# Weight conversion of a one-core attention and MLP kernel: the shifted first words go through a PSUM bank

## The chip, the cores and the metric

The kernel runs on one core of a Trainium2 chip. The metric is the device time of one execution in microseconds (us); smaller is better. PE is TensorE (matmuls), DVE is VectorE, ACT is ScalarE, POOL is GpSimd, SP is the engine that only issues transfers.

## The reference

```python
q_s = exp(q - max(q, -1)); q_s /= sum(q_s, -1) + 1e-9         # 8 batches, 8 heads, 576 rows, 64 wide
k_s = exp(k - max(k, 2));  k_s /= sum(k_s, 2) + 1e-9
x = q_s @ (k_s.T @ v)                                          # heads side by side: (8, 576, 512)
xn = (x - mean(x)) / sqrt(var(x) + 1e-6) * g_ln
x = x + relu(xn @ w_ch1) @ w_ch2                               # w_ch1 (512, 2048), w_ch2 (2048, 512): float64
# then 4 heads of causal attention on x, the two best of 4 by a gate weighted, each through wo
```

What matters here is that the two MLP weights arrive as float64, while the engines compute in float32. Each weight has to be turned into a pair of float32 halves (a rounded high part and the rest) before its matmuls.

## The kernel before

**Weights.** The class `Wide` takes the float64 weights as pairs of int32 words. One block is 128 partitions by 512 values (512 KB); there are 32 blocks, two for each of the 16 slices `f` of the hidden layer (`w1_f`, `w2_f`). A block is loaded by SP into `wraw` (L230) and goes through seven pieces (`pieces`, L234 to L271):

- `size` (ACT, L246): the second word, scaled as a float32, gives `w_t`.
- `shift` (DVE, L250): `w_t` shifted left by 3, SBUF to SBUF, in place.
- `rest` (ACT, L253): the first word as a number, in place in `wraw`.
- `sign` (DVE, L256): the sign bit of the second word is put to `w_t`: two SBUF inputs, SBUF output.
- `whole` (POOL, L260): the rest is added, as an integer.
- `big` (ACT, L263) and `small` (DVE or POOL, L267): the two halves that the matmuls use.

`w_t` has 4 buffers, `wraw` has 4.

**Stages.** 24 blocks (f 0 to 11) are converted in the first stage, together with the attention of batches 0 and 1 in units of two heads (units 0 to 7: `k`, `q`, `km`, `sm`, `pkm`, `pq`, `pkv`, `po`), two layer norms for each of the two batches (`pmu`, `pvar`, `xc`, `xhl`), and the 24 MLP steps of batch 0. A step is 12 matmuls into `psh` (L174), a split into halves `hh` by ACT (L708) and DVE (L711), and 12 matmuls into four `acc` banks; after the last step of a half row block DVE adds `acc` to `xT` (L729). The other 8 blocks (f 12 to 15) are converted in a later round, near 636 to 713 us, while the MLP of batches 6 and 7 runs.

**Order.** In the first stage a planner (`plan`) orders all engines: every piece is an `Op` with an engine, a cost in ns and what it depends on, and takes places in rings (buffers). Of the ops that could start soonest on an engine it takes the one with the earliest due time. An op that takes the ring `y` makes the ops up to its release due at once (`rush`). The order that comes out is then fixed on PE, DVE, ACT and POOL; each engine works strictly in that order. In the later rounds a scheduler of the language orders the engines.

**PSUM.** `psy` gives a bank out of two with the tag `y`; at the start it also hands out three of the `acc` banks in turn, until the first layer norm has read its mean (`spare.clear`). The attention's transposes and products and the layer norm's means live in these banks.

```python
c0 = A(0, ACT, 520, g(0), [at.get(("w", k - 1, 0)), ld])
c1 = A(1, DVE, 340, g(1), [c0])
c2 = A(2, ACT, 520, g(2), [c0])
c3 = A(3, DVE, 600, g(3), [c1])
```

Of the kernel before, what the change touches and what calls it, by code (L numbers as in the profile page):

```python
# [9 lines left out]
I32 = mybir.dt.int32  # L10
U32 = mybir.dt.uint32
AF = mybir.ActivationFunctionType
ALU = mybir.AluOpType
# [116 lines left out]
def tile_kernel(ctx: ExitStack, tc: tile.TileContext, q, k, v, g_ln, w1, w2, w_gate, wq, wk, wv, wo, out):  # L130
    nc = tc.nc
    w1, w2 = w1.bitcast(I32), w2.bitcast(I32)
    B, H, S, D = q.shape
    DM = H * D
# [21 lines left out]
    def raw(ap):  # L156
        return ap.bitcast(F32)
# [15 lines left out]
    def mm(o, lhsT, rhs, start, stop):  # L173
        nc.tensor.matmul(o, lhsT, rhs, start=start, stop=stop)  # L174
# [39 lines left out]
    class Wide:  # L214
# [18 lines left out]
        def pieces(self):  # L233

            r, h, lo = self.now()
            n = self.at
            self.at += 1
            low, high = r[:, :, 0], r[:, :, 1]  # L240
            box = []

            def size():
                t = self.pool_t.tile([P, DM], I32, tag="t", name="w_t", bufs=TB)
                box.append(t)
                nc.scalar.activation(t.bitcast(F32), high.bitcast(F32), AF.Copy, scale=REBASE)  # L246

            def shift():
                t = box[0]
                nc.vector.tensor_scalar(t, t, 3, None, op0=ALU.logical_shift_left)  # L250

            def rest():
                nc.scalar.activation(low, low.bitcast(U32), AF.Copy, scale=2.0 ** -29)  # L253

            def sign():
                nc.vector.scalar_tensor_tensor(box[0], high, -0x80000000, box[0], op0=ALU.bitwise_and,  # L256
                                               op1=ALU.bitwise_or)

            def whole():
                nc.gpsimd.tensor_tensor(box[0], box[0], low, op=ALU.add)  # L260

            def big():
                nc.scalar.activation(h, box[0].bitcast(F32), AF.Copy)  # L263

            def small():
                eng = nc.vector if n in CDVE else nc.gpsimd
                eng.tensor_tensor(lo, box[0].bitcast(F32), raw(h), op=ALU.subtract)  # L267
                while len(self.tiles) < min(n + 1 + self.ahead, len(self.blocks)):
                    self.load()

            return size, shift, rest, sign, whole, big, small  # L271

        def now(self):
# [44 lines left out]
    def psy(name):  # L318
        if spare:

            spare.append(spare.pop(0))
            if spare[-1] is not None:
                return ps_acc.tile([P, 512], F32, tag=spare[-1], name=name)
        return ps_y.tile([P, 512], F32, tag="y", name=name)
# [5 lines left out]
    def unit_pool(n):  # L330
        return ap0 if n in (2, 3) else ap
# [7 lines left out]
    for i in range(NPR):  # L339
        t = unit_pool(i).tile([P, NCH, 2, D + 2], F32, tag=f"v{i}", name=f"v{i}", bufs=1)  # L340
        nc.gpsimd.memset(t[:, :, :, D:], 1.0)
        vbuf.append(t)
        t = unit_pool(i).tile([P, P], F32, tag=f"kvw{i}", name=f"kvw{i}", bufs=1)
        nc.gpsimd.memset(t, 0.0)
        kvwhole.append(t)
    for i in range(2):
        t = ap.tile([P, 2, P], F32R, tag=f"kv{i}", name=f"kv{i}", bufs=1)
# [475 lines left out]
    def start():  # L823


        PE_, ACT, DVE, POOL, SP = ENG.PE, ENG.Activation, ENG.DVE, ENG.Pool, ENG.SP
        ops, at, live = [], {}, []

        def add(name, eng, cost, fn, deps=(), lat=LAT):
            op = at[name] = Op(eng, cost, fn, deps, lat)  # L830
            ops.append(op)
            return op
# [165 lines left out]
        for k in range(nblocks):  # L998
            box = []
            live.append(box)  # L1000
            A = lambda nm, eng, cost, fn, deps: add(("w", k, nm), eng, cost, fn, deps)

            def one(i, box=box):
                if not box:
                    box.extend(wide.pieces())
                box[i]()

            g = lambda i, one=one: (lambda: one(i))
            ld = add(("w", k, "ld"), SP, 1450, wide.load, [at.get(("w", k - 1, "ld"))], lat=1100)
            c0 = A(0, ACT, 520, g(0), [at.get(("w", k - 1, 0)), ld])  # L1010
            c1 = A(1, DVE, 340, g(1), [c0])
            c2 = A(2, ACT, 520, g(2), [c0])
            c3 = A(3, DVE, 600, g(3), [c1])
            c5 = c4 = A(4, POOL, 1220, g(4), [c2, c3])
            c6 = A(6, ACT, 520, g(5), [c4])
            c7 = A(7, *((DVE, 600) if k in CDVE else (POOL, 1220)), g(6), [c6, at.get(("w", k - 1, 7))])
            c0.take("t", c7)
            ld.take("raw", c5)
# [8 lines left out]
        for n, st in enumerate(steps):  # L1027
            u = Step(*st)
            b, h, f, f0, f1 = st[:5]
            live.append(u.__dict__)  # L1030
            A = lambda nm, eng, cost, fn, deps: add(("mm", n, nm), eng, cost, fn, deps)
# [57 lines left out]
    spare.extend(SPARE)  # L1089
    n0 = len(traced())  # L1090
    start()
    in_order(traced()[n0:])

# [521 lines left out]
```

## Time and profile before

| | us |
|---|---|
| median of 3 runs | 1356.46 (1353.22 to 1361.91) |
| the profiled execution | 1351.34 |
| its span, first to last instruction | 1349.5 |
| PE / DVE / ACT / POOL busy | 1298.5 / 872.3 / 688.5 / 342.9 |

The profile is of one execution. Its span is shorter than its time by 1.84 us, which lie around the instructions. Busy times of PE are modelled for overlapping matmuls; the granted clock says how fast TensorE was allowed to run.

### The profile page before, as it was taken

How to read it: one execution, taken by the hardware profiler on the slowest of the kernel's cores; microseconds unless marked ns; L12 is line 12 of the kernel's file. 1: busy time of each engine (PE TensorE's matmuls, PEld its weight loads, DVE VectorE, ACT ScalarE, POOL GpSimd, SP SyncE). 2: the span in 40 equal slices, each digit the busy share in tenths (PEclk: the TensorE clock that was granted, in tenths of full speed). 3: DMA queues.
4: the chain of work that ended last, by engine and by line, in shares of the span. 5: the costliest groups of instructions: out<-in, count | busy, mean ns of one | idle time of the engine just before them, and what ended most of it. 6: DMA issues, size and time to landing. Idle time of an engine off the chain costs nothing.

```text
span 1349.5 us, 26838 instructions
## 1 busy us (share of the span) xinstructions
PE 1298.5 (96%) x9932; PEld 1257.0 (93%) x9932; DVE 872.3 (65%) x2570; ACT 688.5 (51%) x1802; POOL 342.9 (25%) x445
## 2 busy tenths in 40 slices
PE   5788999999999999999999999999999999999997
PEld 3677999999999999999999999999999999999995
DVE  7997565745646655556472247777768676776785
ACT  7786343434334433334442135656666656565666
POOL 5867123122131221212240002111212111121211
PEclk9799999999999999999999999999999999999999
DMA  9764232331322323315212033323232332422021
GB/s 229 217 189 123 76 112 56 117 95 45 110 75 98 89 70 110 76 53 156 64 34 47 1 96 111 105 82 107 89 91 90 93 96 66 121 79 85 23 67 56
DMA packets 136771, 124.84 MB, mean 93 GB/s; under 512 B 84160, under 2 KB 124096, under 8 KB 133056
## 3 DMA queue, kind: packets, MB, share of 16 engines
q1 hardware_dynamic: 126176, 97.16, 25.9%
q10 hardware_dynamic: 10464, 25.95, 5.2%
q8 instruction: 79, 1.29, 0.4%
q14 instruction: 52, 0.43, 0.1%
HBM read 74.07 MB, written 35.39 MB: 81 GB/s over the span
## 4 chain that ended last, share of the span: by engine, by line
PE 79%; DVE 9%; DMA 4%; ACT 3%; issue 2%; SPq 1%; POOL 1%; ACTq 0%; DVEq 0%; POOLq 0%
PE psh L174 25%; PE acc L174 19%; PE psqk L174 7%; PE psc L174 7%; PE pssc L174 4%; PE py L174 4%; PE psv L174 4%; PE pso L174 3%; PE pst L1400 2%; DMA q<-in_q_dram 2%; PE po L174 1%; DVE w_t L256 1%; DVE w_t L250 1%; DMA wraw<-in_moe_w_ch_dram 1%; DMA k<-in_k_dram 1%
## 5 line engine op out<-in xcount | busy, mean ns | idle before, releaser
L174 PE MATMUL psh<-xhl,w 128*128 128x288 f32 x3072 | 473.3, 299 | 2.2 <-DVE xhl L661 1.6
L174 PEld LDWEIGHTS psh<-xhl,w 128*128 128x128 f32 x3072 | 430.9, 190 | 5.8 <-DVE xhl L661 2.3
L174 PE MATMUL acc<-hh,w 128*128 128x288 f32 x2400 | 373.3, 300 | 9.6 <-DVE hh L711 8.7
L174 PEld LDWEIGHTS acc<-hh,w 128*128 128x128 f32 x2400 | 336.8, 190 | 15.2 <-DVE hh L711 12.4
L711 DVE SCALAR_TENSOR_TENSOR hh<-psh,hh 128x288 fp32r<-128x288 f32 x200 | 90.4, 452 | 153.4 <-ACT hh L708 152.3
L708 ACT ACTIVATE hh<-psh 128x288 fp32r<-128x288 f32 x200 | 81.8, 409 | 163.3 <-PE psh L174 155.6
L1388 POOL TENSOR_SCALAR sm<-sm,st,lg 128x128 f32<-128x128 f32 (+3 forms) x128 | 80.8, 641 | 273.7 <-DVE st L1385 99.3
L174 PE MATMUL psqk<-x,wqk 128*128 128x288 f32 x768 | 112.6, 298 | 0.5 <-DVE lg L1288 0.3
L174 PEld LDWEIGHTS psqk<-x,wqk 128*128 128x128 f32 x768 | 104.7, 188 | 1.8 <-PE pst L1400 0.8
L174 PE MATMUL psc<-hb,w 128*128 128x288 f32 x672 | 100.5, 299 | 0.0
L1376 ACT ACTIVATE sm<-sm,st 128x128 f32<-128x128 f32 (+2 forms) x144 | 83.7, 583 | 18.3 <-DVE st L1368 16.4
L174 PEld LDWEIGHTS psc<-hb,w 128*128 128x128 f32 x672 | 92.4, 189 | 0.3
L1419 ACT ACTIVATE aTh<-pst 128x128 fp32r<-128x128 f32 (+5 forms) x254 | 79.3, 335 | 24.3 <-PE pst L1400 11.9
L1368 DVE CUSTOM_DVE_ANT_0 sm<-pssc,mask 128x128 f32<-128x128 f32 (+2 forms) x144 | 67.6, 482 | 32.7 <-PE pst L1400 20.4
L1420 DVE TENSOR_TENSOR aTl<-pst,aTh 128x384 fp32r<-128x384 f32 (+4 forms) x222 | 82.0, 382 | 10.1 <-ACT aTh L1419 7.5
L473 POOL TENSOR_TENSOR qe<-q,sm 128x320 f32<-128x320 f32 x64 | 47.9, 769 | 99.5 <-PE pkv L512 93.7
L608 POOL TENSOR_TENSOR sq<-sq 128x288 f32<-128x288 f32 x45 | 37.0, 822 | 116.1 <-ACT sq L636 114.0
L174 PE MATMUL py<-aTh,vv 128*128 128x320 f32 (+4 forms) x228 | 58.4, 275 | 1.6 <-DVE yf L1472 0.9
L174 PE MATMUL pssc<-k,q 128*128 128x128 f32 (+3 forms) x256 | 58.0, 326 | 0.5 <-DVE st L1368 0.5
L422 POOL TENSOR_TENSOR q<-q,sm 128x640 f32<-128x640 f32 x28 | 35.8, 1278 | 85.7 <-DVE sm L419 85.5
L260 POOL TENSOR_TENSOR w_t<-w_t,wraw 128x512 int32<-128x512 int32 x32 | 46.1, 1443 | 40.6 <-issue 11.7
L419 DVE TENSOR_REDUCE sm<-q 128x10 f32<-128x640 f32 x32 | 26.1, 816 | 44.5 <-DMA q<-in_q_dram 44.5
(173 smaller groups left out, 2123.2 us busy)
## 6 DMA issues: line engine op xcount, KB each, us to landing
wraw<-in_moe_w_ch_dram SPq DMA_DIRECT2D x32, 512.0 KB, 3.8
xn_d<-xhl ACTq DMA_DIRECT2D x14, 1152.0 KB, 4.9
xhl<-xn_d SPq DMA_DIRECT2D x14, 1152.0 KB, 5.2
xp_d<-xT ACTq DMA_DIRECT2D x16, 576.0 KB, 3.5
k<-k SPq DMA_DIRECT2D x32, 288.0 KB, 3.5
k<-in_k_dram SPq DMA_DIRECT2D x32, 256.0 KB, 2.8
q<-in_q_dram SPq DMA_DIRECT2D x32, 256.0 KB, 3.6
out_dram<-ot SPq DMA_DIRECT2D x32, 256.0 KB, 2.0
```

The lines of the kernel that those rows point to most:

```text
L174: nc.tensor.matmul(o, lhsT, rhs, start=start, stop=stop)
L260: nc.gpsimd.tensor_tensor(box[0], box[0], low, op=ALU.add)
L422: nc.gpsimd.tensor_tensor(self.q3, self.q3, self.sm[:, 0, :, None].to_broadcast([P, 2 * NCH, D]), op=ALU.subtract)
L473: nc.gpsimd.tensor_tensor(self.qe[:, :, j, :], self.qt[:, j], self.sm[:, 2, j * NCH:(j + 1) * NCH, None].to_broadcast([P, NCH, D]), op=ALU ...
L608: nc.gpsimd.tensor_tensor(self.t, self.t, self.sq[:, c], op=ALU.add)
L708: nc.scalar.activation(self.hh[:, 0], self.ps, AF.Relu)
L711: nc.vector.scalar_tensor_tensor(self.hh[:, 1], self.ps, 0.0, raw(self.hh[:, 0]), op0=ALU.max, op1=ALU.subtract)
L1368: nc.vector.tensor_tensor_reduce(out=sm[:m, c0:c1], in0=o_, in1=msk, scale=1.0, scalar=3e38 if n == 0 else st[:m, j, 0:1], op0=ALU.add, op ...
L1376: nc.scalar.activation(sm[:m, :w], sm[:m, :w], AF.Exp, bias=st[:m, j, last:last + 1], scale=-1.0, accum_out=st[:m, j, 2:3])
L1388: nc.gpsimd.tensor_scalar(sm[:m, :w], sm[:m, :w], st[:m, j, 3:4], self.gate()[:, j:j + 1], op0=ALU.mult, op1=ALU.mult)
L1419: nc.scalar.activation(oh, from_, AF.Copy)
L1420: nc.vector.tensor_tensor(ol, from_, raw(oh), op=ALU.subtract)
```

## The change

The shifted word no longer goes back to `w_t` in SBUF but to a bank of PSUM taken with `psy`, and the sign is put to it from there; the result goes to `w_t` as before. The planner's cost of the shift is 600 instead of 340, and the shift takes a place in the ring `y` until the sign has read it.

```diff
             def shift():
-                t = box[0]
-                nc.vector.tensor_scalar(t, t, 3, None, op0=ALU.logical_shift_left)
+                box.append(psy(f"pw{n}")[:, :DM].bitcast(I32))
+                nc.vector.tensor_scalar(box[1], box[0], 3, None, op0=ALU.logical_shift_left)
...
             def sign():
-                nc.vector.scalar_tensor_tensor(box[0], high, -0x80000000, box[0], op0=ALU.bitwise_and,
+                nc.vector.scalar_tensor_tensor(box[0], high, -0x80000000, box[1], op0=ALU.bitwise_and,
                                                op1=ALU.bitwise_or)
...
-            c1 = A(1, DVE, 340, g(1), [c0])
+            c1 = A(1, DVE, 600, g(1), [c0])
             c2 = A(2, ACT, 520, g(2), [c0])
             c3 = A(3, DVE, 600, g(3), [c1])
+            c1.take("y", c3)
```

No operation is added or removed, but the planner's order moves. In the first MLP steps, DVE works from the first split `hh` to the third in this order before:

```order
L711 SCALAR_TENSOR_TENSOR hh<-psh,hh 128x288
L250 TENSOR_SCALAR w_t<-w_t 128x512
L256 SCALAR_TENSOR_TENSOR w_t<-wraw,w_t 128x512
L711 SCALAR_TENSOR_TENSOR hh<-psh,hh 128x288
L419 TENSOR_REDUCE sm_684<-q_539 128x10
L250 TENSOR_SCALAR w_t<-w_t 128x512
L630 TENSOR_TENSOR xc<-xT,pmu 128x576 x2
L256 SCALAR_TENSOR_TENSOR w_t<-wraw,w_t 128x512
L250 TENSOR_SCALAR w_t<-w_t 128x512 x2
L256 SCALAR_TENSOR_TENSOR w_t<-wraw,w_t 128x512
L711 SCALAR_TENSOR_TENSOR hh<-psh,hh 128x288
```

And so now (`pw` is the PSUM bank of a block):

```order
L711 SCALAR_TENSOR_TENSOR hh<-psh,hh 128x288
L419 TENSOR_REDUCE sm_676<-q_518 128x10
L630 TENSOR_TENSOR xc<-xT,pmu 128x576 x2
L711 SCALAR_TENSOR_TENSOR hh<-psh,hh 128x288
L250 TENSOR_SCALAR pw_724<-w_t 128x512
L256 SCALAR_TENSOR_TENSOR w_t<-wraw,pw_724 128x512
L250 TENSOR_SCALAR pw_745<-w_t 128x512
L256 SCALAR_TENSOR_TENSOR w_t<-wraw,pw_745 128x512
L250 TENSOR_SCALAR pw_765<-w_t 128x512
L256 SCALAR_TENSOR_TENSOR w_t<-wraw,pw_765 128x512
L711 SCALAR_TENSOR_TENSOR hh<-psh,hh 128x288
```

Each sign now stands right behind its shift, one pair has moved ahead of the first split, and the mean's subtraction (L630) stands ahead of the second one.

On PE, around the sixth MLP step, the order before was (`po` is an attention product of unit 4, the first `acc` rows belong to `w2_5`, the last to `w2_6`):

```order
L174 MATMUL po_929<-qT_847,kvw_136 128x288
L174 MATMUL psh<-xhl,w_6_522 128x288 x12
L174 MATMUL acc_657<-hh,w_5_165 128x288 x3
L174 MATMUL acc_658<-hh,w_5_165 128x288 x3
L174 MATMUL acc_659<-hh,w_5_165 128x288 x3
L174 MATMUL acc_660<-hh,w_5_165 128x288 x3
L174 MATMUL po_991<-qT_847,kvw_136 128x288
L174 MATMUL acc_657<-hh,w_6_523 128x288 x3
```

And now:

```order
L174 MATMUL acc_679<-hh,w_5_165 128x288 x3
L174 MATMUL acc_680<-hh,w_5_165 128x288 x3
L174 MATMUL acc_681<-hh,w_5_165 128x288 x3
L174 MATMUL acc_682<-hh,w_5_165 128x288 x3
L174 MATMUL psh<-xhl,w_6_528 128x288 x12
L174 MATMUL po_990<-qT_794,kvw_136 128x288
L174 MATMUL po_1006<-qT_794,kvw_136 128x288
L507 MATMUL pq_1009<-ident,qe_983 128x112 x4
L174 MATMUL acc_679<-hh,w_6_529 128x288 x3
```

The two products of the unit, which stood on both sides of a `psh` and an `acc` group, now stand one behind the other, with unit 5's transposes behind them.

In the later round four of the eight blocks moved. Before, the shifts and signs of the first four stood apart, two near 637 to 641 us and the fourth around the norm's `pvar`:

```order
L647 SCALAR_TENSOR_TENSOR sq<-pvar,sq 128x288
L250 TENSOR_SCALAR w_t<-w_t 128x512
L648 SCALAR_TENSOR_TENSOR pvar<-sq 128x288
L256 SCALAR_TENSOR_TENSOR w_t<-wraw,w_t 128x512
L652 SCALAR_TENSOR_TENSOR xc<-xc,g_sb,pvar 128x288 x4
```

Now the first four stand together on DVE, behind the second norm's sum of squares, which ran at 685 us before:

```order
L615 TENSOR_TENSOR lnsum<-sq,lnsum 128x288
L250 TENSOR_SCALAR pw_8120<-w_t 128x512
L256 SCALAR_TENSOR_TENSOR w_t<-wraw,pw_8120 128x512
L250 TENSOR_SCALAR pw_8166<-w_t 128x512
L711 SCALAR_TENSOR_TENSOR hh<-psh,hh 128x288
L256 SCALAR_TENSOR_TENSOR w_t<-wraw,pw_8166 128x512
L250 TENSOR_SCALAR pw_8209<-w_t 128x512
L256 SCALAR_TENSOR_TENSOR w_t<-wraw,pw_8209 128x512
```

They take their bank only when the norm's tiles have left one.

## Rows read from the trace of the kernel before

**Rows 1.** The page: busy times; PE, DVE and TensorE's clock in 40 slices.
```profile
PE 1298.5 (96%) x9932; PEld 1257.0 (93%) x9932; DVE 872.3 (65%) x2570; ACT 688.5 (51%) x1802; POOL 342.9 (25%) x445
...
PE   5788999999999999999999999999999999999997
...
DVE  7997565745646655556472247777768676776785
...
PEclk9799999999999999999999999999999999999999
```

**Rows 2.** Busy by stretch (us; instructions in brackets): PE, PEld, DVE, ACT, POOL, clock, DMA, GB/s.
```profile
47.30:119.90 72.60, 60.00 (x395) 55.99 (x395) 70.12 (x105) 52.84 (x131) 51.38 (x39) 0.88 0.56 173
...
130.00:140.00 10.00, 10.00 (x90) 9.64 (x89) 4.00 (x10) 3.62 (x9) 3.43 (x4) 1.00 0.29 68
```

**Rows 3.** Chain that ended last, 47.3 to 119.9 us, by line.
```profile
by line: DVE w_t L256 16.9%; DVE w_t L250 13.6%; issue 13.6%; DVE w L267 8.6%; PE acc L174 6.7%; ACT q L456 6.4%; DVE hh L711 4.6%; DVE xhl L661 3.8%; DVE sm L467 3.1%; PE psh L174 2.8%; ACT w L263 2.3%; ACT wraw L253 2.1%; DVE sm L464 2.0%
```

**Rows 4.** Waits, 10 to 125 us: total, times, longest.
```profile
PE acc L174 <- DVE hh L711: 7.4, 6, 2.7
```

**Rows 5.** DVE groups, 47.3 to 119.9 us: busy us, mean ns; idle before.
```profile
L256 DVE SCALAR_TENSOR_TENSOR w_t<-wraw,w_t 128x512 int32<-128x512 int32 x18 | 20.4, 1136 | 0.3
L250 DVE TENSOR_SCALAR w_t<-w_t 128x512 int32<-128x512 int32 x18 | 15.9, 888 | 0.0
L267 DVE TENSOR_TENSOR w<-w_t,w 128x512 fp32r<-128x512 f32 x10 | 10.2, 1017 | 0.0
```

**Rows 6.** Single lines: ns least/median/greatest, first and last start.
```profile
L250 DVE TENSOR_SCALAR w_t<-w_t x32: 365/428/1545, 18.6 to 704.1; 128x512 int32<-128x512 int32 x32
L256 DVE SCALAR_TENSOR_TENSOR w_t<-wraw,w_t x32: 675/894/1772, 19.3 to 707.3; 128x512 int32<-128x512 int32 x32
L711 DVE SCALAR_TENSOR_TENSOR hh<-psh,hh x200: 395/457/466, 51.0 to 790.2; 128x288 fp32r<-128x288 f32 x100
L729 DVE TENSOR_TENSOR xT<-xT,acc x72: 392/447/456, 88.9 to 794.9; 128x288 f32<-128x288 f32 x72
L648 DVE SCALAR_TENSOR_TENSOR pvar<-sq x16: 454/466/770, 41.4 to 691.6; 128x288 f32<-128x288 f32 x16
```

**Rows 7.** DVE group, whole span: 512 columns from one PSUM and one SBUF input.
```profile
L1420 DVE TENSOR_TENSOR aTl<-pst,aTh 128x512 fp32r<-128x512 f32 x2 | 1.4, 688 | 0.3 <-ACT aTh L1419 0.3
```

**Rows 8.** DVE and POOL in order of time: start us, us.
```profile
68.64 1.52 DVE L250 TENSOR_SCALAR w_t<-w_t 128x512 int32<-128x512 int32 x1
70.20 1.65 DVE L256 SCALAR_TENSOR_TENSOR w_t<-wraw,w_t 128x512 int32<-128x512 int32 x1
...
68.26 1.62 POOL L260 TENSOR_TENSOR w_t<-w_t,wraw 128x512 int32<-128x512 int32 x1 [1.75 <-ACT w_t L246]
69.84 1.46 POOL L267 TENSOR_TENSOR w<-w_t,w 128x512 fp32r<-128x512 f32 x1
```

**Rows 9.** L250, then L256, 18 to 47.3 us: length, DVE busy, clock, DMA, GB/s.
```profile
18.00:47.30 29.30, 3.01 (x7) 0.92 0.92 244
...
18.00:47.30 29.30, 5.52 (x6) 0.92 0.92 244
```

**Rows 10.** Groups of ACT and POOL, 47.3 to 119.9 us; L554: 10 to 125 us.
```profile
L456 ACT ACTIVATE q<-q,sm 128x64 f32<-128x64 f32 x20 | 6.7, 338 | 0.3 <-DVE sm L451 0.3
...
L456 ACT ACTIVATION_READ_ACCUMULATOR q<-q,sm 128x1 f32 x20 | 3.8, 190 | 0.0
...
L260 POOL TENSOR_TENSOR w_t<-w_t,wraw 128x512 int32<-128x512 int32 x18 | 26.2, 1455 | 21.6 <-ACT wraw L253 6.8 <-DVE w_t L256 4.7 <-ACT w_t L246 3.4
...
L554 ACT ACTIVATE xT<-po 128x288 f32<-128x288 f32 x12 | 4.7, 409 | 2.2 <-PE po L174 2.2
```

**Rows 11.** Busy by stretch in the later round, columns as in rows 2.
```profile
680.00:700.00 20.00, 20.00 (x153) 20.00 (x152) 11.22 (x23) 10.81 (x22) 6.21 (x6) 1.00 0.08 30
700.00:720.00 20.00, 18.84 (x135) 17.79 (x134) 14.48 (x20) 8.46 (x17) 9.39 (x7) 1.00 0.37 80
```

## The prediction

> **What bounds the kernel now.** First the page [rows 1]: PE is busy 96% of the span and shows a 9 in nearly every slice. The only slices below are the first four and the last. So time can be won or lost where PE is not yet full, in the first 120 us or so, or where a change makes it wait later. Then the busy times by stretch [rows 2]: from 130 us on PE is busy all the time at a clock of 1.00. From 47.3 us (the first MLP step is running) to 119.9 us (the `acc` banks of the second half block have been added) DVE is busy 70.12 of 72.60 us, PE 60.00 at a mean clock of 0.88, ACT 52.84, POOL 51.38. DVE is the full engine there. The waits say the same [rows 4]: PE's `acc` matmuls wait 7.4 us for the split `hh`, which stands behind the weights in DVE's queue. The chain of that stretch [rows 3] gives 16.9% to the sign (L256) and 13.6% to the shift (L250): 12.3 and 9.9 us, 22.1 together.
>
> Next, why these two are so long. Eighteen pairs run in the stretch, 20.4 us of signs and 15.9 us of shifts, means 1136 and 888 ns [rows 5]. But the least of a sign is 675 ns and of a shift 365 ns, and the greatest 1772 and 1545 [rows 6]. In the order of time [rows 8] the shift at 68.64 us takes 1.52 us and ends at 70.16, within 0.3 us of the end of POOL's add, which had begun at 68.26 with 1.62 us; the sign behind it, 1.65 us, ends at 71.85 after POOL's 69.84 to 71.30. DVE instructions that read or write PSUM with one side do not show this: `hh` (L711, one input in PSUM) stays between 395 and 466 ns over 200 instances, the add of `acc` (L729) between 392 and 456 over 72 [rows 6], while POOL is busy 51.38 of 72.60 us in the same stretch. So the long ones are waits for POOL, met by DVE where both sides of a shift, or both inputs of a sign, are in SBUF.
>
> **The change, part by part.** No operation goes or comes; two change where they write and read.
>
> *The sign.* One input in SBUF, one in PSUM. The nearest row has 512 columns and the same mix: 688 ns [rows 7]. I take 0.69 us; from below 0.675 us (the least sign now), from above 1.14 (the mean now, if the wait for POOL stays).
>
> *The shift.* SBUF to PSUM. The trace has one DVE line that writes PSUM, L648, 288 columns: 454, 466 and 770 ns [rows 6]; its 770 has two SBUF inputs. From 466 ns at 288 columns and 688 at 512 [rows 7] I take 0.69 us. Bounds: 0.365 us (the least now) and 1.54 us (the longest now).
>
> An undisturbed shift thus becomes longer, from about 0.43 to 0.69 us [rows 6, 7]. [...]
>
> *Sum on DVE in the stretch.* 36.36 us now (20.45 + 15.91 [rows 5]) against 18 x 1.38 = 24.8: 11.5 us less. The new order has the same DVE instructions between the first split and the last `acc` add of the stretch (18 shifts, 18 signs, 10 L267, 14 splits), but for one pair of tiny ones.
>
> *How much is on the path.* 22.1 of the 36.36 us are on the chain [rows 3, 5], 61%. So 11.5 x 0.61 = **7.0 us** off. The rest, 4.5 us, lies where ACT, PE or a transfer ends the wait.
>
> *The first six pairs*, before 47.3 us: 3.01 + 5.52 = 8.53 us now [rows 9] against 6 x 1.38 = 8.3. **0.**
>
> *Waits for a bank.* The shift now needs one of two banks, and all of DVE stands behind a shift that waits: the splits `hh` among it, for which PE waits. Of the 18 shifts seven come next after a tile of attention or norm in the banks, the others after another block's, whose sign the plan puts next to its shift. On PE the two `po` of unit 4 now stand together; the second waits for ACT's copy of the first, 0.41 us [rows 10], then unit 5's transposes. I take **+1.0 us** for all of it. From below 0; from above seven waits of a copy behind a group of five exps, 5 x 0.53 = 2.6 us each [rows 10], 18.5 us.
>
> *Waits that move.* L267, ten times on DVE, still has both inputs in SBUF: 1017 ns mean against 0.68 us for an undisturbed two-input one [rows 5, 6], 3.4 us of waits. If the stretch shrinks by 7 us, POOL fills 51.38 of 65.6 in place of 72.6, 78% for 71%: **+0.3 us.**
>
> *TensorE's clock.* [...] With fewer gaps I give back 6.9 x 0.12 = **-0.8 us**.
>
> *The later round.* Four of the eight pairs move to where the second norm has left its bank, near 685 to 695 us. DVE has 8.8 us idle in 680 to 700, POOL 13.8 [rows 11], against 4 x 1.38 = 5.5 us and four POOL adds. Their matmuls are twelve MLP steps away there. PE loses 1.16 us there now, in 700 to 720 us, where DVE is busiest. Pairs without waits for POOL help, the crowding hurts: **0**, bounds -1.2 and +2.
>
> Sum: -7.0 + 1.0 + 0.3 - 0.8 = **-6.5 us**. The span goes from 1349.5 to 1343.0, with the 1.84 us around it to 1344.8. The profiled execution (1351.34) was 5.1 us under the median of the runs (1356.46), and below the fastest of them; I put the same difference on the median: **1350.0 us**.
>
> **Rivals.** All times are for the median.
>
> First, the whole saving arrives: DVE is alone the bound, 11.5 us go, and the clock's 0.8. 1356.5 - 12.3 = 1344.2. For it: the other engines have 52.8, 51.4 and PE 60.0 x 0.88 = 52.8 us of work in the stretch [rows 2], all under the 58.6 that DVE would keep. Against: ACT's exps hold 6.4% of the chain already [rows 3].
>
> Second, the time is taken over: ACT, POOL's adds and the order of `hh` against the steps end the waits at almost the old times, and 1 us remains: 1355.5. For it: 13.6% of the chain is "issue", time for which the view names no wait [rows 3], and chains block by block run over ACT, DVE, ACT, POOL, ACT. Against: the steps' splits come closer together in the new order, one by one.
>
> Third, slower: the banks. Seven shifts wait 2.6 us each behind ACT's exps [rows 10], with all of DVE behind them: 18.5 - 7.0 = +11.5, 1368.0. It decides from 1.0 us a shift (7.0 / 7). For it: the two banks are shared with all of attention and with `pvar`, which is kept from the mean to the last scaling. Against: the plan counts the banks, and puts the sign next to the shift.
>
> Fourth, the change doesn't do what it says: POOL's waits are only handed on to the next DVE instruction with two SBUF sides, and the shift pays 0.26 us more. 4.7 us x 0.61 = +2.9, 1359.4. Against: ten L267 and few others are left to take over the waits of 36. [...]
>
> **How the numbers follow.** Forecast 0.46, first rival 0.16, second 0.23, third 0.09, fourth 0.06. The forecast's own spread is some 4 us either way, and the median of a few runs moves as the three runs did (1353 to 1362). The range 1340 to 1361 holds the forecast, the first, second and fourth rivals but for their ends, and leaves out most of the third. A measurement of this kernel tells about 1% from no change, 13.6 us: under 1342.9 lies only the better part of the first rival, 0.11; over 1370.0 the worse half of the third, 0.05; the rest is 0.84.
>
> **What the profile would show.** Right: signs and shifts at 0.65 to 0.72 us with almost no spread, while POOL is as busy as before; DVE about 25 us for the 18 pairs; POOL's L260 shorter than its mean of 1.46 us now [rows 10]; the last `acc` add of the stretch 5 to 8 us earlier, and the same lead at the end. Wrong in the term on the path: pairs short, but DVE idle in front of L711 with ACT or PE as the releaser. Wrong in the banks: DVE idle in front of L250 released by ACT's L497, L534 or L554, or PE idle in front of `po` and `pq` released by DVE. Wrong altogether: shifts or signs still up to 1.5 us. A loss after 130 us, near 690 to 715 us above all, would show as PE idle in front of `acc` there.

## The result: 17 us faster, and 12 us when measured again

| us | before | changed kernel | ratio, 95% interval |
|---|---|---|---|
| median of the runs | 1355.48 | 1338.41 | 0.9875 (0.984 to 0.991) |
| measured again, beside the later experiments | 1354.6 | 1341.23 | 0.9909 (0.9889 to 0.993) |
| span of the profiled execution | 1349.5 | 1335.6 | |

The forecast was 1350.0, 6.5 us off. The first measurement gives 17.1 us, the second 1354.6 x 0.0091 = 12.3 us (9.5 to 15.0). Both lie clearly above the forecast; the second, with more runs of the kernel before beside it, is the one the experiments are compared with. It came out faster, as forecast, and the pairs got shorter as forecast; the 6.5 us were 0.38 of the first gain and 0.53 of the second.

The page of the changed kernel, the lines that answer to [rows 1]:

```profile
PE 1295.4 (97%) x9932; PEld 1254.7 (94%) x9932; DVE 856.9 (64%) x2570; ACT 688.1 (52%) x1802; POOL 334.3 (25%) x445
...
PE   5789999999999999999999999999999999999997
...
DVE  6996654655547646555473167777778676776785
...
PEclk9899999999999999999999999999999999999999
```

DVE lost 15.4 us of busy time and POOL 8.6, with the same number of instructions. The fourth slice of PE has become a 9.

The changed lines in the changed kernel, ns least/median/greatest, to hold against [rows 6]:

```profile
L250 DVE TENSOR_SCALAR pw<-w_t x32: 673/685/696, 19.3 to 691.2; 128x512 int32<-128x512 int32 x32
...
L256 DVE SCALAR_TENSOR_TENSOR w_t<-wraw,pw x32: 668/686/690, 20.0 to 693.0; 128x512 int32<-128x512 int32 x32
...
L267 DVE TENSOR_TENSOR w<-w_t,w x14: 677/922/1785, 32.4 to 698.5; 128x512 fp32r<-128x512 f32 x14
```

The spread of shift and sign is gone. L267, which keeps two SBUF inputs, still reaches 1785 ns. The groups of the same 18 pairs, 46.2 to 110.4 us, answer to [rows 5] (busy us, mean ns; idle before):

```profile
L256 DVE SCALAR_TENSOR_TENSOR w_t<-wraw,pw 128x512 int32<-128x512 int32 x18 | 12.4, 687 | 1.0
L250 DVE TENSOR_SCALAR pw<-w_t 128x512 int32<-128x512 int32 x18 | 12.3, 684 | 0.6 <-ACT xT L554 0.5
L267 DVE TENSOR_TENSOR w<-w_t,w 128x512 fp32r<-128x512 f32 x10 | 11.4, 1156 | 0.9 <-ACT w L263 0.8
```

24.7 us for the 18 pairs; the prediction said 24.8. That the work of POOL is still beside them is seen in the order of time (start us, us), to hold against [rows 8]:

```profile
66.56 0.68 DVE L250 TENSOR_SCALAR pw<-w_t 128x512 int32<-128x512 int32 x1
66.77 1.32 POOL L260 TENSOR_TENSOR w_t<-w_t,wraw 128x512 int32<-128x512 int32 x1 [2.01 <-ACT lnsum L612]
67.28 0.69 DVE L256 SCALAR_TENSOR_TENSOR w_t<-wraw,pw 128x512 int32<-128x512 int32 x1
```

POOL's add runs from 66.77 to 68.09; the shift began before it and the sign begins within it, and none of the three is lengthened (the add's 1.32 us is near its median in this kernel, 1.31).

Busy time by stretch in the changed kernel, columns as in [rows 2], to hold against [rows 2, 11]:

```profile
47.30:119.90 72.60, 64.13 (x474) 59.51 (x474) 64.83 (x112) 57.60 (x142) 55.47 (x47) 0.95 0.62 190
...
120.00:130.00 10.00, 10.00 (x89) 9.64 (x88) 4.04 (x10) 3.61 (x9) 3.43 (x4) 1.00 0.25 61
680.00:700.00 20.00, 19.93 (x150) 19.69 (x149) 13.70 (x24) 13.64 (x26) 12.29 (x9) 1.00 0.34 95
700.00:720.00 20.00, 20.00 (x154) 20.00 (x153) 6.12 (x13) 4.87 (x11) 0.00 (x0) 1.00 0.24 51
```

In the old stretch PE now runs 474 matmuls instead of 395, at a mean clock of 0.95 instead of 0.88, and it is full from 120 us on. The row at 130 us of [rows 2], DVE 4.00, ACT 3.62, POOL 3.43, stands here at 120 us almost digit for digit: from there on the program is about 10 us earlier. The `acc` adds of the first two half row blocks (L729), first and last start, before and then after, say it directly: 119.5 has become 110.0, **9.5 us**. (In a second profile of the changed kernel, the run `again` below, the last add starts at 111.7; one profile gives this lead to within some 2 us.)

```profile
L729 DVE TENSOR_TENSOR xT<-xT,acc x8: 441/444/450, 88.9 to 119.5; 128x288 f32<-128x288 f32 x8
```
```profile
L729 DVE TENSOR_TENSOR xT<-xT,acc x8: 440/444/450, 84.2 to 110.0; 128x288 f32<-128x288 f32 x8
```

Of the rest of the 13.9 us of span, 1.16 us are PE's idle time at 700 to 720 us [rows 11], which is gone, and 2.4 us lie in 140 to 700 us, where the two kernels do the same up to 636 us: PE is busy 555.6 of 560 us before and 558.1 after. That part is no gain of the change: the kernel with the new order alone, below, has 557.9 there and no shorter time.

One trap: the chain of waits that ended last reaches back only to 91.37 us in the changed kernel. Its first pieces, cut at 92 us (start us, us):

```profile
91.37 0.09 issue
91.47 0.70 DVE w_t L256
```

Its shares can therefore not be set against [rows 3].

### The profile page after: what moved, and what is told of

Its sections match the earlier page's. It is cut to its first block, busy times and chain, and to the rows that moved or that the text cites. A ratio compares the mean times of both kernels' runs of the same rounds, so it can differ in the third digit from the quotient of the medians.

```text
span 1335.6 us, 26853 instructions
## 1 busy us (share of the span) xinstructions
PE 1295.4 (97%) x9932; PEld 1254.7 (94%) x9932; DVE 856.9 (64%) x2570; ACT 688.1 (52%) x1802; POOL 334.3 (25%) x445
## 4 chain that ended last, share of the span: by engine, by line
PE 83%; DVE 3%; DMA 2%; ACT 2%; POOL 1%; issue 1%; SPq 0%; ACTq 0%; POOLq 0%; DVEq 0%
PE psh L174 27%; PE acc L174 20%; PE psqk L174 7%; PE psc L174 7%; PE pssc L174 4%; PE py L174 4%; PE psv L174 4%; PE pso L174 3%; PE pst L1401 2%; PE po L174 2%; PE pkv L174 1%; DMA q<-in_q_dram 1%; DMA wraw<-in_moe_w_ch_dram 1%; PE pq L507 1%; PE pst L1450 1%
## 5 line engine op out<-in xcount | busy, mean ns | idle before, releaser
L174 PE MATMUL acc<-hh,w 128*128 128x288 f32 x2400 | 369.4, 298 | 5.3 <-DVE hh L711 4.9
L1377 ACT ACTIVATE sm<-sm,st 128x128 f32<-128x128 f32 (+2 forms) x144 | 83.7, 583 | 17.9 <-DVE st L1369 16.2
L1420 ACT ACTIVATE aTh<-pst 128x128 fp32r<-128x128 f32 (+5 forms) x254 | 79.2, 334 | 24.6 <-PE pst L1401 12.3
L1421 DVE TENSOR_TENSOR aTl<-pst,aTh 128x384 fp32r<-128x384 f32 (+4 forms) x222 | 81.9, 381 | 10.2 <-ACT aTh L1420 7.7
L473 POOL TENSOR_TENSOR qe<-q,sm 128x320 f32<-128x320 f32 x64 | 45.2, 726 | 101.3 <-PE pkv L512 96.1
L174 PE MATMUL psv<-wvg,x 128*128 128x260 f32 (+1 forms) x384 | 54.3, 285 | 0.0
L1401 PE MATMUL pst<-ident,sm 128*128 128x128 f32 x320 | 53.1, 277 | 0.0
```

The source lines that it names most:

```text
L473: nc.gpsimd.tensor_tensor(self.qe[:, :, j, :], self.qt[:, j], self.sm[:, 2, j * NCH:(j + 1) * NCH, None].to_broadcast([P, NCH, D]), op=ALU ...
L1377: nc.scalar.activation(sm[:m, :w], sm[:m, :w], AF.Exp, bias=st[:m, j, last:last + 1], scale=-1.0, accum_out=st[:m, j, 2:3])
L1401: nc.tensor.transpose(pt[:kw, kb * m:kb * m + m], sm[:m, kb * P:kb * P + kw], ident[:m, :m])
L1420: nc.scalar.activation(oh, from_, AF.Copy)
L1421: nc.vector.tensor_tensor(ol, from_, raw(oh), op=ALU.subtract)
```

## The experiments

Each was timed beside the kernel before, on the same chip; ratios are to that kernel. Not all runs had the same chip, so runs are set against each other by these ratios, not by their times. A percent is 13.5 us. Three causes were in question: the price of the pairs (placement in a bank), the planner's new order, and the later round. Line numbers in the experiments are up to three higher than in the kernels above.

**order_only.** The changed kernel's cost, ring place and rotation of the banks, but the shift stays in SBUF. In the first stage each engine's order is the changed kernel's, in the later round the old one.

```diff
-                box.append(psy(f"pw{n}")[:, :DM].bitcast(I32))
+                box.append(box[0])
+                if spare:
+                    spare.append(spare.pop(0))
```

> The planned first stage issues in the changed kernel's order (cost 600, the place in the bank ring, the rush), but the shift writes back to SBUF, as before, and the last eight blocks are as before. Placement theory (the time comes from the pairs' price, the order is worth nothing): signs and shifts of the stage still average 0.8 to 1.1 us with single ones to 1.7 us, and the time is 1352 to 1358, within 3 us of the kernel before. Order theory (the sign next to its shift and the rush let PE's steps start earlier, whatever the price): 1341 to 1347.

Measured: 1350.64 against 1351.2, ratio 0.9993 (0.9975 to 1.0011). DVE groups of the kernel before and then of this one, 0 to 140 us:

```profile
L256 DVE SCALAR_TENSOR_TENSOR w_t<-wraw,w_t 128x512 int32<-128x512 int32 x24 | 26.0, 1082 | 0.5
L250 DVE TENSOR_SCALAR w_t<-w_t 128x512 int32<-128x512 int32 x24 | 18.9, 791 | 2.9 <-ACT w_t L246 2.8
```
```profile
L258 DVE SCALAR_TENSOR_TENSOR w_t<-wraw,w_t 128x512 int32<-128x512 int32 x24 | 27.9, 1162 | 0.8
L252 DVE TENSOR_SCALAR w_t<-w_t 128x512 int32<-128x512 int32 x24 | 16.2, 674 | 1.6 <-ACT w_t L246 1.6
```

The pairs cost 44.1 us, against 44.9 before: the new order hardly shortens them, and the time by 0.9 us (-1.5 to 3.4). The order theory, which put the kernel 9 us or more under the one before, falls. (1350.64 lies under the range of the placement theory only because the kernel before was at 1351.2 on this chip; the 3 us between them are kept.)

**front_only** and **late_only.** The bank in the first stage alone (with the new order there), and in the last eight blocks alone (with the old cost and no ring place in the plan).

```diff
-                box.append(psy(f"pw{n}")[:, :DM].bitcast(I32))
+                box.append(psy(f"pw{n}")[:, :DM].bitcast(I32) if not self.ahead else box[0])    # front_only
+                box.append(box[0] if not self.ahead else psy(f"pw{n}")[:, :DM].bitcast(I32))    # late_only
```

> Bank placement and new order in the planned first stage only; the last eight blocks shift in SBUF in the kernel-before's order. Theory that the first stage gives all: 1337 to 1342, the changed kernel's time. Theory that the later round gives 3 us or more (PE's idle time at 700 to 720 us, 1.16 us before, none after, and what follows): 1341 to 1345, with PE idle at 700 to 720 us again.

> The complement: first stage as in the kernel before, bank placement for the last eight blocks only. Theory that the first stage gives all: 1353 to 1357. Theory that the later round gives 3 us or more: 1350 to 1352, with no idle PE at 700 to 720 us.

Measured: front_only 1340.25, ratio 0.9918 (0.9895 to 0.994), 11.1 us (8.1 to 14.2) faster; late_only 1350.04, 0.9991 (0.9972 to 1.0011), 1.2 us (-1.5 to 3.8). The two add up to 12.3 us, the changed kernel's 12.3; that they meet so closely is chance, as each carries some 3 us either way. The first stage carries the gain. The rows of the later round, of order_only (bank nowhere) and then of late_only:

```profile
700.00:720.00 20.00, 19.13 (x139) 18.23 (x138) 13.20 (x20) 7.81 (x16) 7.61 (x6) 1.00 0.37 80
```
```profile
700.00:720.00 20.00, 20.00 (x153) 20.00 (x152) 9.14 (x17) 7.78 (x16) 5.47 (x4) 1.00 0.37 81
```

PE's idle time of 0.9 us disappears with the bank, as the second theory said; in front_only, without the bank there, PE idles again, 1.0 us at 690 to 720 us. The time gives that microsecond, 1.2 us, but its interval reaches to 3.8, so the three of the second theory are not excluded.

front_only and order_only have the same order on every engine throughout and differ in the bank of 24 blocks alone. The pairs of front_only, 0 to 140 us, to hold against order_only's above:

```profile
L256 DVE SCALAR_TENSOR_TENSOR w_t<-wraw,pw 128x512 int32<-128x512 int32 x24 | 16.5, 686 | 1.2
L250 DVE TENSOR_SCALAR pw<-w_t 128x512 int32<-128x512 int32 x24 | 16.4, 685 | 3.3 <-ACT w_t L246 1.7 <-ACT kvw L534 0.8 <-ACT xT L554 0.5
```

They take 16.5 + 16.4 = 32.9 us, 11.2 less; the time is 0.75% less, 10.1 us (6.2 to 14.0). So the price of the pairs is shown as the cause. Of each us of DVE time that they gave up, 0.90 us reached the end, but the interval, 0.55 to 1.25, is too wide to tell this from the prediction's 61%; the runs with added work below are for that.

**again** and **bank_old_costs.** The changed kernel once more; and the changed kernel with the old cost of the shift in the plan and without the rush.

```diff
-            c1 = A(1, DVE, 600, g(1), [c0])
+            c1 = A(1, DVE, 340, g(1), [c0])
             c3 = A(3, DVE, 600, g(3), [c1])
             c1.take("y", c3)
+            c1.calm = True
...
-            if ring == "y":
+            if ring == "y" and not op.calm:
```

> The changed kernel once more, beside the runs below. Every theory: 0.985 to 0.992 of the kernel before. If the two parts add up (first stage 0.9918, last eight blocks 0.9991), 0.990 to 0.992; a whole better than that, 0.985 to 0.989, would mean that they help each other.

> Bank placement with the plan's old price of the shift (340) and without the rush of the sign; the bank's place in the ring is still planned. Placement theory: pairs at 0.69 us each and 1336 to 1343, whatever the price in the plan. If placement and new order are needed together (the order pays only where the pairs are short): 1345 to 1352.

Measured: again 0.9909, where the parts alone had made 0.9909. bank_old_costs 1344.25, 0.9925 (0.99 to 0.9951), with the pairs at 686 and 683 ns: the bank brings its 10.2 us under another order too. Its median is 1.3 us above the one expected range and 0.8 us under the other, and the difference of 0.16% to the changed kernel is inside both intervals: whether the new order adds a microsecond or two to the bank stays open.

**shift_twice, shift_thrice, size_twice.** How much of an added us of DVE or ACT time arrives? The first two write the shift again to its bank, the third does ACT's first piece twice; all in the first stage alone.

```diff
                 nc.vector.tensor_scalar(box[1], box[0], 3, None, op0=ALU.logical_shift_left)
+                for _ in range(0 if self.ahead else 2):                     # shift_thrice; shift_twice: once
+                    nc.vector.tensor_scalar(box[1], box[0], 3, None, op0=ALU.logical_shift_left)
...
                 nc.scalar.activation(t.bitcast(F32), high.bitcast(F32), AF.Copy, scale=REBASE)
+                if not self.ahead:                                           # size_twice
+                    nc.scalar.activation(t.bitcast(F32), high.bitcast(F32), AF.Copy, scale=REBASE)
```

> The changed kernel with each of the first stage's 24 shifts written twice to its bank: 24 more DVE instructions of 0.69 us, 16.5 us of DVE time, the order else kept. If DVE's time there passes whole to the end: 1338 + 14 to 17 = 1352 to 1355. If it passes by the 61% of the prediction: 1338 + 10 = 1348. If other engines end the waits: below 1344.

> The changed kernel with each of the first stage's 24 shifts written three times: 48 more DVE instructions of 0.69 us, 33 us of DVE time. At 0.8 to 0.9 of DVE's time: 0.991 of before plus 26 to 30 us, 14 to 18 us over the kernel before. At the prediction's 61%: plus 20 us, 8 us over the kernel before.

> The changed kernel with ACT's first step of each of the first stage's 24 blocks done twice: 24 more ACT instructions of about 0.6 us, 14 to 15 us of ACT time. DVE alone the bound: ACT is busy 65 of the 80 us from 40 to 120, so 0 to 4 us more than the changed kernel. If ACT shares the bound (the second rival of the prediction): 7 to 13 us more.

Measured: shift_twice 1.0007 (0.999 to 1.0024), shift_thrice 1.0111 (1.0088 to 1.0135), size_twice 0.9963 (0.9943 to 0.9983). The added groups, 0 to 140 us, of shift_thrice and then of size_twice:

```profile
L252 DVE TENSOR_SCALAR pw<-w_t 128x512 int32<-128x512 int32 x48 | 33.4, 695 | 1.6
```
```profile
L248 ACT ACTIVATE w_t<-wraw 128x512 f32<-128x512 f32 x24 | 16.3, 677 | 0.8
```

Over the changed kernel's 0.9909, shift_thrice costs 2.02%, 27.3 us for 33.4 us of DVE: **0.82** (0.69 to 0.94, from the intervals of both ratios). shift_twice costs 0.98%, 13.3 us for 16.7: 0.80 (0.58 to 1.01). The 61% of the prediction lies outside the first interval, though inside the wider second one; shift_thrice is also 15.0 us over the kernel before, where 14 to 18 were expected at 0.8 to 0.9 and 8 at 61%. size_twice costs 0.54%, 7.3 us (3.4 to 11.2) for 16.3 us of ACT: 0.45, where 0 to 4 us were expected with DVE alone as the bound and 7 to 13 if ACT shares it. So DVE's time counts most in the stage, but ACT's counts too. The run does not tell ACT's full queue from the delay of each block, whose shift has to wait for the doubled piece: DVE's idle time in front of the 24 shifts rose from 3.2 us in the changed kernel to 7.2.

**pad_on, pad_off, pad_on_more, pad_off_more.** Does DVE time count only where it stands on the chain of waits? The kernel before, with three (then six) more shifts by 0 behind four blocks whose pairs stand on its chain, or behind four that do not.

```diff
                 nc.vector.tensor_scalar(t, t, 3, None, op0=ALU.logical_shift_left)
+                for _ in range(3 if n in (13, 14, 15, 19) else 0):          # pad_off; pad_on: 12, 17, 21, 22
+                    nc.vector.tensor_scalar(t, t, 0, None, op0=ALU.logical_shift_left)
```

> The kernel before with three more shifts (by 0, in place) behind the shift of the blocks 12, 17, 21 and 22, counted from 0, whose pairs stand on the chain of waits of before: 12 DVE instructions of 0.43 to 0.9 us, 6 to 10 us of DVE time. By the chain (the prediction's way to count): the whole of it, 6 to 10 us slower. By the queue (all DVE time of the stage counts alike, about 0.8): 5 to 8 us slower.

> The same twelve shifts behind the blocks 13, 14, 15 and 19, whose pairs stand not on the chain of before (of 15 only a part of the shift does). By the chain: 0 to 2 us slower. By the queue: 5 to 8 us slower, as with the blocks on the chain.

> The same six behind blocks 12, 17, 21 and 22 (on the chain of before): 15 to 20 us of DVE time. By the queue and by the chain alike: 11 to 18 us slower.

> The kernel before with six more shifts by 0, in place of three, behind blocks 13, 14, 15 and 19 (off the chain of before): 24 instructions, 15 to 20 us of DVE time. By the queue: 11 to 17 us slower. By the chain: at most half of what the blocks on the chain cost.

| | ratio | slower by, us | added DVE time, us |
|---|---|---|---|
| pad_on | 1.0053 (1.0036 to 1.007) | 7.2 | 9.8 |
| pad_off | 1.0038 (1.0021 to 1.0056) | 5.1 | 8.9 |
| pad_on_more | 1.0083 (1.0063 to 1.0103) | 11.2 | 14.9 |
| pad_off_more | 1.0097 (1.0072 to 1.0123) | 13.1 | 16.2 |

The added groups of pad_on_more and pad_off_more, 0 to 140 us:

```profile
L252 DVE TENSOR_SCALAR w_t<-w_t 128x512 int32<-128x512 int32 x24 | 14.9, 622 | 0.8
```
```profile
L252 DVE TENSOR_SCALAR w_t<-w_t 128x512 int32<-128x512 int32 x24 | 16.2, 675 | 0.8
```

Off the chain the same work costs about as much as on it: 0.81 of its time against 0.75 with six, 0.57 against 0.73 with three. The chain's way to count would have made pad_off 0 to 2 us and pad_off_more at most half of pad_on_more. It falls. The shares are not prices of one us of DVE time, though, since the added shifts also shorten the pairs around them: from 44.9 us before to 39.5 and 39.3 on the chain, but only to 43.5 and 43.0 off it. Net of that the doses are 4.4 and 9.3 us on the chain and 7.5 and 14.3 off it, and they cost 1.6, 1.2, 0.68 and 0.92 of themselves. Time off the chain counts for most of itself; that it counts for as much as time on the chain is not shown.

**no_pool_add.** order_only with POOL's add (L260) left out in the first stage.

```diff
             def whole():
-                nc.gpsimd.tensor_tensor(box[0], box[0], low, op=ALU.add)
+                if self.ahead:
+                    nc.gpsimd.tensor_tensor(box[0], box[0], low, op=ALU.add)
```

> The kernel with the changed order and the shift in SBUF, with GpSimd's add of the low word left out in the first stage (24 adds; the low words are then missing from those weights). If the long shifts and signs are waits for GpSimd: the pairs fall from 1.84 us to 1.3 to 1.6 (the attention's and the low parts' work on GpSimd stays), and the time falls by 5 to 12 us. If they wait for something else (transfers, ACT): the pairs stay near 1.84 us.

Measured: 1334.02, 0.9857 (0.9834 to 0.9881). Its DVE groups, 0 to 140 us, against those of order_only above:

```profile
L258 DVE SCALAR_TENSOR_TENSOR w_t<-wraw,w_t 128x512 int32<-128x512 int32 x24 | 20.3, 845 | 0.8
L252 DVE TENSOR_SCALAR w_t<-w_t 128x512 int32<-128x512 int32 x24 | 11.7, 489 | 3.0 <-ACT w_t L246 3.0
```

With POOL's adds gone, the pairs in SBUF fall from 44.1 to 32.0 us, 1.33 us each, on the way to the 1.10 us of an undisturbed pair (0.43 + 0.68 [rows 6]). So most of what made shifts and signs long, 12.1 of the 17.7 us above 24 x 1.10, were waits for POOL's adds; POOL's other work stayed. The time fell by 18.4 us against order_only, more than expected: L267 on DVE fell too (12.7 to 8.2 us), and each block's way over POOL is shorter by the add, which this run does not separate.

**true_costs and cdve_two.** Two tries at more: the plan's prices nearer to the trace, and two blocks fewer with their low part on DVE.

```diff
-            c1 = A(1, DVE, 600, g(1), [c0])
+            c1 = A(1, DVE, 660, g(1), [c0])          # true_costs; c3 also 660, c7 on DVE 1000 instead of 600
...
-CDVE = (1, 4, 7, 8, 9, 14, 16, 17, 18, 20, 21)
+CDVE = (1, 4, 7, 9, 14, 16, 18, 20, 21)              # cdve_two
```

> The changed kernel with the plan's prices nearer to the trace: 660 in place of 600 for shift and sign, 1000 in place of 600 for the low part on DVE. Placement theory: the order is worth little, within 3 us of the changed kernel. If the order of the stage is what matters: 4 us or more either way.

> The changed kernel with the low part of two more blocks (8 and 17) on GpSimd in place of DVE: DVE has 2.2 us less, GpSimd 2.6 us more. If DVE's time still bounds the stage at 0.8: 0 to 3 us faster. If GpSimd's adds are now late: 1 to 4 us slower.

Measured: 0.9903 (0.9883 to 0.9923) and 0.9904 (0.9881 to 0.9927). Neither can be told from the changed kernel's 0.9909, so no better version is claimed.

## Why the prediction was too small

**Prices: right.** Both were taken as 0.69 us and came as 0.685 and 0.686, without spread (673 to 696 and 668 to 690 ns); in order_only, in the first stage with the same order on every engine but with the shift in SBUF, the means are 0.674 and 1.162. The undisturbed shift became longer, as forecast: 428 ns at the median in SBUF [rows 6], 685 now. It paid all the same, since a shift in SBUF cost 791 ns on the mean of the first stage and a sign 1082, waits included. The reading of the long ones as waits for POOL, met where both sides of a shift or both inputs of a sign are in SBUF, held: without POOL's adds the pairs of 1.84 us fall to 1.33 (no_pool_add), and the rows at 66.56 us show a shift into the bank and a sign from it at 0.68 and 0.69 us beside such an add.

**DVE's sum: right.** 11.5 us were forecast for the 18 pairs, 36.36 - 24.7 = 11.7 came. The first six pairs were put at 0: 8.53 us before, 33.0 - 24.7 = 8.3 after.

**The step that failed** is "How much is on the path": "22.1 of the 36.36 us are on the chain [rows 3, 5], 61%. So 11.5 x 0.61 = 7.0 us off. The rest, 4.5 us, lies where ACT, PE or a transfer ends the wait." The share was too small: added DVE time arrived at 0.82 (0.69 to 0.94), and the time that the pairs gave up at 0.90 in front_only against order_only. Two things in the step were wrong.

The first is the reading of the chain. The 61% counts only pieces that bear the names of shift and sign. Another 13.6% of the stretch, 9.9 us, is called "issue" [rows 3], and the second rival took it as a sign that other engines set the time. Laid beside DVE's own instructions in the kernel before, DVE is at work in all but 0.5 us of it, and in 6.0 us of it a shift or a sign is running. One such place, on the chain and then in the order of time (start us, us):

```profile
52.38 0.04 DVE w_t L256
52.41 0.98 issue
53.40 0.45 DVE hh L711
```
```profile
52.38 1.09 DVE L256 SCALAR_TENSOR_TENSOR w_t<-wraw,w_t 128x512 int32<-128x512 int32 x1
53.40 0.45 DVE L711 SCALAR_TENSOR_TENSOR hh<-psh,hh 128x288 fp32r<-128x288 f32 x1
```

The sign runs for 1.09 us until `hh` follows, and the chain gives it 0.04. With the 6.0 us, 28.2 of the 36.36 us are on the chain, 0.78 and no longer 0.61, which lies inside the measured interval.

The second is the reason given for the rest. By the pads, time off the chain is not free: it counts for 0.57 to 0.81 of itself, or 0.68 to 0.92 net of the pairs that got shorter. The better row was already there, DVE busy 70.12 of 72.60 us [rows 2]: that what stands off the chain in a queue that full pushes back what stands on it is the likely reason, argued and not shown by a run of its own.

With 0.82 the 11.9 us of the 24 pairs give 9.8 us, with 0.90 10.7; the first stage measured 11.1 (8.1 to 14.2).

**Bank waits, +1.0: not settled.** DVE's idle time in front of the 24 shifts was 2.9 us before. After, it is 3.2, of which ACT's copies that free a bank account for 1.3 (0.8 and 0.5); in the second profile of the same kernel, `again`, it is 4.5, of which 2.6:

```profile
L250 DVE TENSOR_SCALAR pw<-w_t 128x512 int32<-128x512 int32 x24 | 16.5, 686 | 3.2 <-ACT w_t L246 1.7 <-ACT kvw L534 0.8 <-ACT xT L554 0.5
```
```profile
L250 DVE TENSOR_SCALAR pw<-w_t 128x512 int32<-128x512 int32 x24 | 16.5, 686 | 4.5 <-ACT kvw L534 2.1 <-ACT w_t L246 1.7 <-ACT xT L554 0.5
```

So the bank waits partly took the place of waits for ACT's first piece, and DVE's idle time there rose by 0.3 us in one profile and 1.6 in the other; the forecast's 1.0 lies between. The third rival, 18.5 us of bank waits, is out.

**Moved waits, +0.3: not more than that.** The ten L267 of the stretch went from 10.2 to 11.4 us, but all eleven of the first stage only from 11.9 to 12.1. DVE's busy time up to the last `acc` add of the two half row blocks fell from 106.9 to 93.3 us, 13.6 us, more than the 11.9 of the pairs, so on balance nothing was handed on, and the fourth rival is out. (Its 4.7 us were 18 x 0.26, the price of an undisturbed shift that goes from 0.43 to 0.69 us; that rise came, 428 to 685 ns, but with it the waits went.) **Clock, -0.8:** its 6.9 us are 6.7 + 2.8% of 72.6 us [rows 3], its 0.12 what the mean clock of 0.88 lacks to 1.00 [rows 2]; no run shows the term by itself. The runs showed the stretch at 0.95 in place of 0.88. From 40 to 60 us both kernels have 0.74; from 60 to 80 us it is 0.74 before, with PE busy 14.02 of 20 us, and 1.00 after, with 16.67. That fewer gaps raise it was the author's estimate and is not shown: in the first 40 us the clock is 1.00 in both kernels, with PE busy only 20.94 and 23.53 us. What it gave is contained in 0.82. **Later round, 0:** late_only leaves -1.5 to 3.8 us, and PE's 1.16 us of idle time are gone, the better end of its bounds.

**The rivals.** The first, the whole saving arrives, gave 1344.2, a ratio of 0.991, and is what the second measurement shows. That its number fits is partly luck: its reason, DVE alone as the bound, is only mostly right (0.82 and not 1, with ACT at 0.45), and it left out the later round. The second, time taken over by ACT and POOL, is out in its size by both measurements, though ACT does share in setting the time.

**Where it stays open.** The first measurement (17.1 us, 12.2 to 21.7) and the second (12.3 us, 9.5 to 15.0) overlap; which is nearer for a given chip was not settled. Shares of 0.82 and of 0.90 both fit the first stage, and how much of ACT's 0.45 is its queue was not separated.

## What to carry to other kernels

Where an engine's queue is as full in a stretch as DVE's was here, 97% busy, price a saving by the queue, near its whole (0.82 of added DVE time arrived here, 0.90 of the saved), and use the chain of waits to find the engine, not to discount the saving. Before a share of the chain is used, lay its "issue" pieces beside the engine's own instructions: here most of them were the engine at work. Check the share by adding a known dose of work to that engine and to its neighbour. A wide spread between least and greatest of one DVE line (365 to 1545 ns for the shift, 675 to 1772 for the sign), beside a busy GpSimd, was here mostly time waited and not worked: giving one side of the instruction a place in PSUM bought a fixed price, here 0.69 us, which paid because the mean with waits, 1.87 us a pair in the first stage, was above 2 x 0.69. A reordering that comes with such an edit should be timed alone before it is given credit.

## What the runs showed that was not expected

The waits reach instructions of almost no work: L467, 128 x 10 values in SBUF, takes 151 to 1105 ns in the changed kernel, and the longest, at 72.26 us, ends with POOL's add of 72.01 to 73.33:

```profile
L467 DVE TENSOR_SCALAR sm<-sm x32: 151/165/1105, 12.2 to 619.2; 128x10 f32<-128x10 f32 x32
```

POOL's side got shorter too. Its add fell from 1457 to 1347 ns on the mean of the 24 of the first stage, 2.7 us of POOL time that the prediction left out of its sum:

```profile
L260 POOL TENSOR_TENSOR w_t<-w_t,wraw 128x512 int32<-128x512 int32 x24 | 35.0, 1457 | 26.7 <-ACT wraw L253 11.1 <-DVE w_t L256 4.7 <-ACT w_t L246 3.4
```
```profile
L260 POOL TENSOR_TENSOR w_t<-w_t,wraw 128x512 int32<-128x512 int32 x24 | 32.3, 1347 | 21.1 <-ACT wraw L253 11.3 <-DVE w_t L256 7.7 <-ACT lnsum L612 2.0
```

Most of that came with the new order: in order_only, with the pairs still in SBUF, the add takes 1371 ns, and in front_only 1350. What the bank alone is worth to POOL is seen in its busy time in these two runs, from 0 to 800 us: 239.45 us in order_only and 234.41 in front_only, 5.0 us less, of which only 0.5 us are in these adds.

PE's idle time between 140 and 700 us moved with no relation to the edits: 1.9 us in the changed kernel, 2.3 in the same kernel profiled again, 4.4 before, 2.1 in order_only, 5.4 in bank_old_costs. Differences of 2 us between two profiled spans should not be read as the work of a change.
